# A one-token decode layer on one core: Tile framework against a recorder, load pieces of 16 to 32 KB against 16 to 64 KB per partition, softmax per kv head against per two kv heads

## The chip, the cores and the metric

The kernel runs on one core of one Trainium2 chip. A core has five engines with an instruction stream each: PE (TensorE, matrix products, writes to PSUM), DVE (VectorE), ACT (ScalarE), POOL (GpSimd) and SP (SyncE, which here only issues DMAs). Sixteen DMA engines move data between HBM and SBUF, the on-chip memory of 128 partitions. The metric is device microseconds of one execution; lower is better. Before the change it is 229.72 us, the median of 3 runs (229.62 to 229.88).

## The reference

One token passes through a parallel layer: layer norm, attention over the last 4096 positions of a cache with 32 query heads on 4 kv heads, and a gated MLP. All is float32.

```python
W = min(4096, max(256, Sk // 4))                     # 4096
xn = _layernorm(x)                                   # (1, 1, 1024)
q = (xn @ wq).reshape(B, Sq, 32, 128)                # wq 1024 x 4096
k = repeat(k_cache[:, :, Sk - W:, :], 8)             # 4 kv heads x 4096 x 128
v = repeat(v_cache[:, :, Sk - W:, :], 8)
p = softmax(q k^T * 128 ** -0.5)
a = (p v).reshape(B, Sq, 4096) @ wo                  # wo 4096 x 1024
h = gelu_tanh(xn @ w_gate) * (xn @ w_up)             # both 1024 x 3584
out = x + a + h @ w_down                             # w_down 3584 x 1024
```

Each weight and each cached key and value is used once, so about 94.4 MB pass from HBM to SBUF.

## The kernel before

All loads are issued by SP in one order (`items`, L75 to L79): four pieces of wq, then k, gate, v and up pieces mixed, then four of wo and four of w_down. A piece fills one of four buffers `chunk` of 32 KB per partition (L55, `load`, L88). Piece n + 4 is loaded into the buffer of piece n, so its DMA on SP waits until PE and DVE have read the whole of piece n (L449). A k or v piece holds two kv heads in two DMAs of 16 KB per partition; a gate or up piece has 28 KB; the last two pieces of w_down are cut finer, down to two DMAs of 2 KB per partition (`TAIL`, L30, and `cuts`, L101).

A projection by a vector (q, gate, up) is done in two halves of the rows: `blocks` (L193) gives half of them to PE as products with a stationary operand of 32 columns, of which one holds x, so that four products stand in four strips of 32 PSUM partitions; `add_scaled` (L181) gives the other half to DVE, which multiplies a row of weights by one number per partition and adds it to `part`. `projected` (L210) sums `part` over the partitions on PE, with `unit`. A q piece of 32 KB is thus one row of 4096 for PE and one for DVE.

Keys: `transpose_keys` (L235) transposes 128 x 128 blocks on PE into two PSUM buffers in turn, four blocks at a time, and ACT copies each group of four to `kT`. `scores` (L245) forms a head's scores as 4 strips x 2 x 512, takes the maximum per partition and the exponential, once per kv head. `values` (L261) multiplies by v. `maxima`, `factors`, `normalizers` and `heads` (L289 to L337) join the partial softmaxes and spread the result over `oz`. `gelu`, `gated` and `hidden` (L344 to L381) form the MLP's inner row `hz`.

wo and w_down (`contract`, L393): a tile is 1024 columns in 128 partitions; every second tile goes to PE (`accumulate`, L387, four products of 256 columns in four strips of `out_p`), the others to DVE (`out_part`). `out_part` joins on PE at tile 20 of w_down; the last tiles all go to PE. Then one DVE addition writes `y` in partitions 0, 32, 64 and 96, one DMA from ACT stores it (L453, L454), and the Tile framework closes the program (its instructions stand under L474).

The order of the work on each engine is the order of the code (`manual_schedule`, L58, and the loop from L410); the framework adds the waits.

Of the kernel before, what the change touches and what calls it, by code (L numbers as in the profile page):

```python
# [9 lines left out]
F32 = mybir.dt.float32  # L10
# [3 lines left out]
PSUM = bass.MemoryType.PSUM  # L14
# [4 lines left out]
REP = HQ // HKV  # L19
# [3 lines left out]
NJ = D // (2 * P)  # L23
NB = 512
NA = DF // NB
CO = D // 4
TD = DF // P
GROUP = 8

TAIL = {0: 1, 1: 4}  # L30

MERGE = 20
# [3 lines left out]
STREAM = 8192  # L36


@with_exitstack
def tile_decode_layer(  # L40
    ctx: ExitStack,
    tc: tile.TileContext,
    x: bass.AP,
    k_cache: bass.AP,
    v_cache: bass.AP,
    wq: bass.AP,
    wo: bass.AP,
    w_gate: bass.AP,
    w_up: bass.AP,
    w_down: bass.AP,  # L50
    out: bass.AP,
):
    nc = tc.nc
    consts = ctx.enter_context(tc.tile_pool(name="consts", bufs=1))
    stream = ctx.enter_context(tc.tile_pool(name="stream", bufs=4))  # L55
    work = ctx.enter_context(tc.tile_pool(name="work", bufs=1))
    psum = ctx.enter_context(tc.tile_pool(name="psum", bufs=1, space=PSUM))
    ctx.enter_context(tc.manual_schedule())  # L58


    def paired(w, jj):
        return w[2 * P * jj:2 * P * (jj + 1), :].rearrange("(p r) n -> p (r n)", r=2)


    def window(cache, g):
        return cache[0, g, SK - WIN:, :].rearrange("(p j) d -> p (j d)", p=P)

    def grouped(w, a):  # L70
        return w[P * GROUP * a:min(P * GROUP * (a + 1), w.shape[0]), :].rearrange(
            "(p t) n -> p t n", p=P
        )

    items = [("q", jj) for jj in range(NJ)]  # L75
    items += [("k", 0), ("g", 0), ("v", 0), ("g", 1), ("g", 2), ("g", 3)]
    items += [("k", 1), ("u", 0), ("v", 1), ("u", 1), ("u", 2), ("u", 3)]
    items += [("o", a) for a in range(HQ // GROUP)]
    items += [("d", a) for a in range(-(-TD // GROUP))]  # L79
    source = {  # L80
        "q": lambda i: [paired(wq, i)], "g": lambda i: [paired(w_gate, i)], "u": lambda i: [paired(w_up, i)],
        "k": lambda i: [window(k_cache, 2 * i + g) for g in range(2)],
        "v": lambda i: [window(v_cache, 2 * i + g) for g in range(2)],
        "o": lambda i: [grouped(wo, i)], "d": lambda i: [grouped(w_down, i)],
    }
    loaded = {}

    def load(n):  # L88
        kind, i = items[n]
        chunk = stream.tile([P, STREAM], F32, name="chunk")  # L90
        at = 0
        for src in source[kind](i):
            size = math.prod(src.shape[1:])
            dst = chunk[:, at:at + size]
            at += size
            if len(src.shape) == 3:
                dst = dst.rearrange("p (t n) -> p t n", t=src.shape[1])
            step = TAIL.get(len(items) - 1 - n)
            if step:
                for t in range(0, src.shape[1], step):  # L100
                    cuts = 2 if n == len(items) - 1 and t == src.shape[1] - 1 else 1  # L101
                    for cut in range(cuts):
                        cols = slice(cut * D // cuts, (cut + 1) * D // cuts)
                        nc.sync.dma_start(dst[:, t:t + step, cols], src[:, t:t + step, cols])
            else:
                nc.sync.dma_start(dst, src)
        loaded[kind, i] = chunk


    x_rows = work.tile([NJ, 2 * P], F32, name="x_rows")  # L110
    nc.scalar.dma_start(x_rows, x.rearrange("a b (j p) -> (a b j) p", j=NJ))
    x_out = work.tile([P, CO], F32, name="x_out")
    nc.vector.memset(x_out, 0.0)
    nc.scalar.dma_start(x_out[0:P:32, :], x.rearrange("a b (c n) -> (a b c) n", n=CO))

    ident = consts.tile([P, P], F32, name="ident")
    make_identity(nc, ident)
    avg = consts.tile([P, P], F32, name="avg")
    nc.vector.memset(avg, 1.0 / D)

    xz = consts.tile([P, 2, NJ, 32], F32, name="xz")
    nc.vector.memset(xz, 0.0)
    qz = consts.tile([P, HKV, 32], F32, name="qz")
    nc.vector.memset(qz, 0.0)
    hz = consts.tile([P, TD, 32], F32, name="hz")
    nc.vector.memset(hz, 0.0)
    oz = consts.tile([P, HQ, 32], F32, name="oz")
    nc.vector.memset(oz, 0.0)
    unit = consts.tile([P, 32], F32, name="unit")
    nc.vector.memset(unit, 0.0)  # L130
    nc.vector.memset(unit[:, 0:1], 1.0)

    same = consts.tile([P, 4, 32], F32, name="same")
    nc.vector.tensor_add(same[:, 0, :], ident[:, 0:32], ident[:, 32:64])
    nc.vector.tensor_add(same[:, 1, :], ident[:, 64:96], ident[:, 96:128])
    nc.vector.tensor_add(same[:, 2, :], same[:, 0, :], same[:, 1, :])
    for c in (0, 1, 3):
        nc.vector.tensor_copy(same[:, c, :], same[:, 2, :])


    pick = consts.tile([P, REP, 16], F32, name="pick")
    nc.vector.tensor_copy(pick, same[:, 0, 0:REP].unsqueeze(2).to_broadcast([P, REP, 16]))
    low = consts.tile([P, 16], F32, name="low")
    nc.vector.reduce_sum(low, ident.rearrange("p (h s) -> p s h", s=16), axis=AX.X)

    def small(name):
        return psum.tile([P, NB], F32, name=name, tag="tp", bufs=2)

    def layer_norm():
        xt_p = small("xt_p")  # L150
        for r in range(2):
            nc.tensor.transpose(
                xt_p[:, r * NJ:(r + 1) * NJ], x_rows[:, r:2 * P:2], ident[:NJ, :NJ]
            )
        xt = work.tile([P, 2 * NJ], F32, name="xt")
        nc.vector.tensor_copy(xt, xt_p[:, :2 * NJ])
        st = work.tile([P, 8], F32, name="st")
        nc.vector.reduce_sum(st[:, 0:1], xt, axis=AX.X)
        mean_p = small("mean_p")
        nc.tensor.matmul(mean_p[:, 0:1], avg, st[:, 0:1], start=True, stop=True)  # L160
        nc.vector.tensor_copy(st[:, 1:2], mean_p[:, 0:1])
        xc = work.tile([P, 2 * NJ], F32, name="xc")
        nc.vector.tensor_scalar(xc, xt, st[:, 1:2], None, op0=ALU.subtract)
        sq = work.tile([P, 2 * NJ], F32, name="sq")
        nc.vector.tensor_mul(sq, xc, xc)
        nc.vector.reduce_sum(st[:, 2:3], sq, axis=AX.X)
        var_p = small("var_p")
        nc.tensor.matmul(var_p[:, 0:1], avg, st[:, 2:3], start=True, stop=True)
        nc.vector.tensor_scalar(st[:, 3:4], var_p[:, 0:1], EPS, None, op0=ALU.add)
        nc.scalar.activation(st[:, 4:5], st[:, 3:4], AF.Sqrt)  # L170

# [7 lines left out]
        )  # L179

    def add_scaled(total, w, factor, first):  # L181

        if first:
            nc.vector.tensor_scalar(total, w, factor, None, op0=ALU.mult)  # L184
        else:
# [292 lines left out]
```

## Time and profile before

| What | us or share |
|---|---|
| device time, median of 3 runs | 229.72 |
| span of the profiled execution, first to last instruction | 228.1 |
| time outside the span (median less span) | 1.6 |
| PE busy, 1096 matrix instructions | 126.9 (56%) |
| DVE busy, 103 instructions | 97.0 (43%) |
| ACT busy, 57 instructions | 33.8 (15%) |
| data moved by DMA | 94.53 MB |
| granted TensorE clock, mean | 0.79 |

Sums over engines do not bound the time: PE, DVE and the DMA engines work side by side. The page cuts the span in 40 slices and gives for each the busy share of every engine and of the DMA engines; a table of windows gives the same for any stretch. The waits of SP tell when a load could not be issued because its buffer was still being read. The profile has no separate time for the profiled execution, so its span of 228.1 us and 1.6 us around it stand for it.

### The profile page before, as it was taken

To read this page: it belongs to the slowest core of one execution; us is meant where nothing else is said; L and a number is where in the kernel's file an instruction comes from. 1 tells how busy PE (TensorE), PEld (TensorE's weight loads), DVE (VectorE), ACT (ScalarE), POOL (GpSimd) and SP (SyncE) were. 2 spreads that over 40 slices of the span, in tenths; PEclk is the share of its full clock that TensorE was granted. 3 is DMA by queue.
4 is the path that set the end of the run, shared out by engine and by line. 5 is a ranking of instruction groups with operands and counts; after the bars stand their busy time and mean duration, and the time that the engine had idled before them with its cause. 6 is when DMAs were issued, how large, how long until landed. Compare 5 with 4: busy or idle time off the path is not lost.

```text
span 228.1 us, 2497 instructions
## 1 busy us (share of the span) xinstructions
PE 126.9 (56%) x1096; PEld 62.8 (28%) x1096; DVE 97.0 (43%) x103; ACT 33.8 (15%) x57; POOL 0.7 (0%) x6
## 2 busy tenths in 40 slices
PE   1160623567939874169806985384895426062754
PEld 1110100154436540017305472110481202021321
DVE  7340724510110564260380327966717356292600
ACT  2000000035065310006416350000000000000000
POOL 1000000000000000000000000000000000000000
PEclk9999999979776998556975899959776655555879
DMA  7999999999999999999999999999999999999990
GB/s 277 455 402 431 460 431 402 428 459 410 424 425 450 410 442 425 413 427 450 415 419 458 417 429 435 422 455 419 417 448 428 414 448 437 419 431 411 418 380 36
DMA packets 4787, 94.53 MB, mean 414 GB/s; under 512 B 541, under 2 KB 553, under 8 KB 1193
## 3 DMA queue, kind: packets, MB, share of 16 engines
q1 hardware_dynamic: 4752, 94.37, 97.0%
q8 instruction: 8, 0.13, 0.2%
q10 hardware_dynamic: 24, 0.01, 0.0%
q14 instruction: 3, 0.02, 0.0%
HBM read 94.38 MB, written 0.00 MB: 414 GB/s over the span
## 4 chain that ended last, share of the span: by engine, by line
DMA 56%; PE 24%; DVE 11%; ACT 5%; issue 2%; SPq 0%; ACTq 0%; DVEq 0%
DMA chunk<-in_A_k_cache 22%; DMA chunk<-in_A_wo 15%; DMA chunk<-in_B_w_down 15%; PE kt_p L241 10%; DMA chunk<-in_A_wq 5%; PE o_p L278 3%; DVE part L186 3%; PE s_p L250 3%; PE out_p L389 3%; PE acc_q L196 2%; DVE out_part L186 2%; DVE m L253 2%; ACT p L256 2%; ACT kT L242 1%; ACT pT L273 1%
## 5 line engine op out<-in xcount | busy, mean ns | idle before, releaser
L186 DVE SCALAR_TENSOR_TENSOR part<-chunk,xz,part 128x3584 f32<-128x3584 f32 (+1 forms) x9 | 37.1, 4126 | 29.4 <-DMA chunk<-in_A_wq 17.8
L241 PE MATMUL kt_p<-ident,chunk 128*128 128x128 f32 x128 | 25.5, 374 | 15.4 <-ACT kT L242 12.3
L242 ACT ACTIVATE kT<-kt_p 128x512 f32<-128x512 f32 x32 | 18.8, 596 | 68.9 <-PE kt_p L241 68.4
L196 PE MATMUL acc_q<-chunk,xz 128*32 128x512 f32 x64 | 14.2, 1040 | 23.7 <-DMA chunk<-in_A_wq 23.7
L241 PEld LDWEIGHTS kt_p<-ident,chunk 128*128 128x128 f32 x128 | 20.2, 192 | 25.2 <-ACT kT L242 15.9
L389 PE MATMUL out_p<-chunk,hz 128*32 128x256 f32 x160 | 14.7, 528 | 16.2 <-DMA chunk<-in_B_w_down 16.2
L186 DVE SCALAR_TENSOR_TENSOR out_part<-chunk,oz,out_part 128x1024 f32<-128x1024 f32 x15 | 19.3, 1285 | 9.7 <-DMA chunk<-in_A_wo 9.3
L389 PE MATMUL out_p<-chunk,oz 128*32 128x256 f32 x128 | 14.2, 621 | 15.3 <-DMA chunk<-in_A_wo 15.3
L196 PE MATMUL acc_g<-chunk,xz 128*32 128x512 f32 x56 | 10.5, 785 | 9.6 <-DMA chunk<-in_B_w_gate 9.6
L253 DVE TENSOR_REDUCE m<-s_p 128x1 f32<-128x1024 f32 x4 | 4.9, 1222 | 23.3 <-PE s_p L250 23.3
L186 DVE SCALAR_TENSOR_TENSOR out_part<-chunk,hz,out_part 128x1024 f32<-128x1024 f32 x8 | 10.3, 1285 | 9.2 <-DMA chunk<-in_B_w_down 8.9
L389 PEld LDWEIGHTS out_p<-chunk,hz 128*32 128x32 f32 x160 | 6.7, 146 | 24.6 <-DMA chunk<-in_B_w_down 12.3
L389 PEld LDWEIGHTS out_p<-chunk,oz 128*32 128x32 f32 x128 | 5.5, 164 | 23.2 <-DMA chunk<-in_A_wo 18.0
L196 PEld LDWEIGHTS acc_q<-chunk,xz 128*32 128x32 f32 x64 | 2.5, 158 | 34.2 <-DMA chunk<-in_A_wq 23.3
L196 PE MATMUL acc_u<-chunk,xz 128*32 128x512 f32 x56 | 9.3, 708 | 3.1 <-DMA chunk<-in_B_w_up 3.1
L250 PE MATMUL s_p<-kT,qz 128*32 128x512 f32 x64 | 10.1, 709 | 0.0
L278 PE MATMUL o_p<-chunk,pT 128*32 128x128 f32 x256 | 7.8, 274 | 1.9 <-ACT pT L273 1.9
L184 DVE TENSOR_SCALAR part<-chunk,xz 128x3584 f32<-128x3584 f32 (+1 forms) x3 | 6.5, 2169 | 3.9 <-DMA chunk<-in_A_wq 3.9
L278 PEld LDWEIGHTS o_p<-chunk,pT 128*32 128x32 f32 x256 | 6.7, 110 | 2.8 <-ACT pT L273 2.8
L196 PEld LDWEIGHTS acc_g<-chunk,xz 128*32 128x32 f32 x56 | 2.1, 125 | 16.2 <-DMA chunk<-in_B_w_gate 12.2
L256 ACT ACTIVATE p<-s_p,negm 128x1024 f32<-128x1024 f32 x4 | 4.5, 1114 | 8.3 <-DVE negm L254 8.3
L350 DVE TENSOR_TENSOR t_sb<-g_sb 128x512 f32<-128x512 f32 (+1 forms) x2 | 1.4, 686 | 9.9 <-ACT g_sb L349 9.9
(93 smaller groups left out, 73.7 us busy)
## 6 DMA issues: line engine op xcount, KB each, us to landing
chunk<-in_A_wq SPq DMA_DIRECT2D x4, 4096.0 KB, 30.8
chunk<-in_A_wo SPq DMA_DIRECT2D x4, 4096.0 KB, 27.8
chunk<-in_B_w_gate SPq DMA_DIRECT2D x4, 3584.0 KB, 17.8
chunk<-in_B_w_up SPq DMA_DIRECT2D x4, 3584.0 KB, 16.7
chunk<-in_A_k_cache SPq DMA_DIRECT2D x4, 2048.0 KB, 26.9
chunk<-in_A_v_cache SPq DMA_DIRECT2D x4, 2048.0 KB, 28.6
chunk<-in_B_w_down SPq DMA_DIRECT2D x2, 4096.0 KB
chunk<-in_B_w_down SPq DMA_DIRECT2D x2, 2048.0 KB, 30.9
```

The source lines that it names most:

```text
L184: nc.vector.tensor_scalar(total, w, factor, None, op0=ALU.mult)
L186: nc.vector.scalar_tensor_tensor(total, w, factor, total, op0=ALU.mult, op1=ALU.add)
L196: nc.tensor.matmul(acc[kind][32 * c:32 * c + 32, b, :], z, w[:, n * NB:(n + 1) * NB], start=start, stop=stop,)
L241: nc.tensor.transpose(t_p[:, jj * P:(jj + 1) * P], kn[:, j * DH:(j + 1) * DH], ident)
L242: nc.scalar.activation(kT[:, i, :], t_p, AF.Copy)
L250: nc.tensor.matmul(s_p[32 * c:32 * c + 32, b, :], qz[:, g, :], kT[:, i, :], start=True, stop=True)
L253: nc.vector.reduce_max(m[:, g:g + 1], s_p, axis=AX.XY)
L256: nc.scalar.activation(p, s_p, AF.Exp, bias=negm[:, g:g + 1], scale=SCALE, accum_out=l[:, g:g + 1])
L273: nc.scalar.activation(pT[:, b].rearrange("p j q -> p (j q)"), t_p, AF.Copy)
L278: nc.tensor.matmul(o_p[32 * c:32 * c + 32, g, :], pT[:, b, jj, 32 * c:32 * c + 32], vn[:, j * DH:(j + 1) * DH], start=(b == 0 and jj == 0) ...
L350: nc.vector.tensor_mul(ts, gs, gs)
L389: nc.tensor.matmul(out_p[32 * c:32 * c + 32, :], z, w[:, c * CO:(c + 1) * CO], start=start, stop=stop)
```

## The change

The Tile framework goes. A class `Program` records every operation with its engine and the boxes (tensor, partitions, range of elements) that it reads and writes, finds for each the latest earlier operation of every other engine or DMA that it has to wait for, and emits the engines' streams with these waits. Engines count on one semaphore each; every DMA has its own. The code's order remains the order on each engine.

Loads go to one ring of 152 KB per partition at fixed places (`pieces`): q, o in two pieces of 64 KB each, gate and up in two of 56 KB, a k piece is one kv head (16 KB), a v piece two kv heads in one DMA (32 KB), w_down 48, 32, 16 KB and four tiles of 4 KB, the last in two halves. A piece is issued on SP as soon as the pieces that lie on its place have been used; pieces are issued in the listed order.

A 64 KB q piece is four rows of 4096: rows 0 and 2 go to PE, 1 and 3 to DVE. Of a gate or up piece one row of four goes to PE, three to DVE. In heads 0 and 1 the copies of key groups 2 and 5 go to DVE, the others to ACT. Scores of two kv heads accumulate in one PSUM bank, 32 rows to a strip (8 heads x 2 kv heads x 2 halves), with `qz` padded so that each product fills its own 8 rows; maximum, exponential and the transposition of the probabilities are then done once for two kv heads. A product of `values` has 512 columns (4 x 128) and `heads` picks each row's own 128 with a masked weight. `hidden` makes its row with two products and a masked sum in place of 36 small products. The program lists 406 matrix operations where it listed 630.

For wo and w_down a PE tile is two products of 512 columns in two strips; tiles alternate between the two pairs of strips. The last two tiles of w_down, `out_part` and the accumulated strips are joined in `final`, in strips of 128 columns x 2 halves, so that the result lies in partitions 31, 32, 95 and 96. Each half has its own addition and two stores, from SP and ACT. At the end SP waits for the four stores and clears the semaphores.

The diff, cut to its core:

```diff
-    stream = ctx.enter_context(tc.tile_pool(name="stream", bufs=4))
...
+RING = 152 * KB
...
+    def emit(self):
...
+        for op in self.ops:
+            engine = self.engines[op["engine"]]
+            waits = [(sems[self.ops[o]["lane"]], self.ops[o]["rank"]) for o in op["waits"]]
+            for sem, value in waits[1:]:
+                engine.wait_ge(sem, value)
+            inst = op["emit"](engine)
+            if waits:
+                inst.wait_op(waits[0][0], waits[0][1], "sem-ge")
...
+    pieces = [
+        ("q", 0, 0, 64), ("q", 1, 72, 64), ("k", 0, 136, 16), ("k", 1, 56, 16), ("g", 0, 0, 56),
+        ("v", 0, 56, 32), ("g", 1, 88, 56), ("k", 2, 0, 16), ("k", 3, 16, 16), ("u", 0, 32, 56),
+        ("v", 1, 0, 32), ("u", 1, 88, 56), ("o", 0, 0, 64), ("o", 1, 64, 64),
+        ("d", (0, 12), 0, 48), ("d", (12, 20), 48, 32), ("d", (20, 24), 80, 16),
+        ("d", (24, 25), 128, 4), ("d", (25, 26), 132, 4), ("d", (26, 27), 136, 4),
+        ("d", (27, 28), 140, 4),
+    ]
...
+    def project(kind, a, on):
+        n = NQ if kind == "q" else NG
+        w = held[kind, a].rearrange("p (r n) -> p r n", r=4)
+        for r in range(4):
+            if r in on:
+                on_pe(kind, xz[:, r, a, :], w[:, r, :], n)
+        for r in range(4):
+            if r not in on:
...
+                add_scaled(part[:, :8 * n], w[:, r, :], xz[:, r, a, 0:1], first)
+        done(kind, a)
...
+    def transpose_keys(g, groups, by):
+        kn = held["k", g]
+        for i in groups:
+            t_p = small()
+            for jj in range(4):
+                j = 4 * i + jj
+                transpose(t_p[:, jj * P:(jj + 1) * P], kn[:, j * DH:(j + 1) * DH], ident[:])
+            copy(kT[:, i, :], t_p[:], by(i))
+        done("k", g)
...
+    def softmax(a):
+        reduce_max(m[:, a:a + 1], s_p[:])
+        scalar_op(negm[:, a:a + 1], m[:, a:a + 1], -SCALE, None, ALU.mult)
+        act(p[:], s_p[:], AF.Exp, bias=negm[:, a:a + 1], scale=SCALE, accum=l[:, a:a + 1])
...
+    def final(half, wide, w, start, stop):
         for c in range(4):
...
+            odd = c % 2
+            mm(
+                acc[32 * c:32 * c + 32, half, :P], wide[:, 31 * odd:31 * odd + 32],
+                w[:, c * P:(c + 1) * P], start, stop,
             )
...
+    project("q", 0, {0, 2})
+    project("q", 1, {0, 2})
+    by = lambda i: "dve" if i in (2, 5) else "act"
+    transpose_keys(0, range(8), by)
+    projected("q")
+    queries()
+    scores(0)
+    transpose_keys(1, range(8), by)
+    scores(1)
+    softmax(0)
+    project("g", 0, {0})
+    transpose_probs()
+    values(0)
...
+    for half in range(2):
+        final(half, unit, out_part[:, half * NQ:(half + 1) * NQ], True, False)
+    copy(acc_sb, out_acc[:], "act")
+    for half in range(2):
+        final(half, half_sel[:, half, :], acc_sb, False, False)
...
+        final(half, hz_last[:, 1, :], w[:, half * NQ:(half + 1) * NQ], False, True)
+        add(y[:, half, :], acc[:, half, :P], x_out[:, half, :])
+        for k, engine in enumerate(("sp", "act")):
+            src = y[31 + 64 * k:33 + 64 * k, half, :]
...
+    for sem in ends:
+        nc.sync.wait_ge(sem, 16)
...
+    nc.sync.sem_clear(range(numbers[0], numbers[-1] + 1))
```

Three places of the streams bear on what follows. The first is SP's stream from the last loads of wq to the first of v; `chunk` is one of the four buffers, the names in brackets are semaphores. Before:

```order
L106 DMA chunk<-in_A_wq 128x8192 x4
L106 DMA chunk<-in_A_k_cache 128x4096 [waits DMAHW1_49,DVE_49,PE_49]
L106 DMA chunk<-in_A_k_cache 128x4096
L106 DMA chunk<-in_B_w_gate 128x7168 [waits DMAHW0_49,DMAHW3_49,DVE_49,PE_49]
L106 DMA chunk<-in_A_v_cache 128x4096 [waits DMAHW4_49,DVE_49,PE_49]
L106 DMA chunk<-in_A_v_cache 128x4096 [waits DMAHW2_49]
```

Now, from the second piece of wq on, with `ring` the one buffer and `s_dve`, `s_pe` the engines' counts:

```order
L192 DMA ring<-in_A_wq 128x16384
L192 DMA ring<-in_A_k_cache 128x4096
L192 DMA ring<-in_A_k_cache 128x4096 [waits s_dve]
L192 DMA ring<-in_B_w_gate 128x14336 [waits s_pe]
L192 DMA ring<-in_A_v_cache 128x2x4096 [waits s_pe]
L192 DMA ring<-in_B_w_gate 128x14336
```

The first load of v waited for the reader of a wq piece four pieces back; now it lies on part of the place of k's head 1 (56 to 72 KB), so it waits for PE's last transposition of that head.

The second place is DVE's stream around the keys of heads 0 and 1. Before, two rows for the last two wq pieces, then the queries and the first softmax:

```order
L186 SCALAR_TENSOR_TENSOR part<-chunk,xz,part 128x4096 [waits DMAHW4_49,DVE_49]
L186 SCALAR_TENSOR_TENSOR part<-chunk,xz,part 128x4096 [waits DMAHW5_49,DVE_49]
L223 COPY qz<-q_p 128x2x8 [waits PE_49] x2
L253 TENSOR_REDUCE m<-s_p 128x1 [waits PE_49]
L254 TENSOR_SCALAR negm<-m 128x1 [waits DVE_49]
```

Now, with `tp` a PSUM buffer of transposed keys:

```order
L186 SCALAR_TENSOR_TENSOR part<-ring,xz,part 128x4096 [waits s_dma5,s_dve]
L186 SCALAR_TENSOR_TENSOR part<-ring,xz,part 128x4096 [waits s_dve]
L159 COPY kT<-tp 128x512 [waits s_pe] x2
L159 COPY rows_sb<-acc 128x512 [waits s_pe]
L159 COPY qz<-tp 128x8 [waits s_pe]
L159 COPY qz<-tp 128x8 x3
L159 COPY kT<-tp 128x512 [waits s_pe] x2
L174 TENSOR_REDUCE m<-s_p 128x1 [waits s_pe]
```

Both DVE rows of the second wq piece now wait for one landing (`s_dma5`), and two copies of transposed keys of each head stand on DVE behind them.

The third place is the end of PE's stream. Before, the last three tiles of w_down, each a product of 256 columns in four strips:

```order
L389 MATMUL out_p<-chunk,hz 32x256 [waits DMAHW7_49]
L389 MATMUL out_p<-chunk,hz 32x256 x3
L389 MATMUL out_p<-chunk,hz 32x256 [waits DMAHW0_49]
L389 MATMUL out_p<-chunk,hz 32x256 x3
L389 MATMUL out_p<-chunk,hz 32x256 [waits DMAHW1_49]
L389 MATMUL out_p<-chunk,hz 32x256
L389 MATMUL out_p<-chunk,hz 32x256 [waits DMAHW2_49]
L389 MATMUL out_p<-chunk,hz 32x256
```

Now, from tile 25 of w_down on:

```order
L134 MATMUL out_acc<-ring,hz 32x512 [waits s_dma516]
L134 MATMUL out_acc<-ring,hz 32x512
L134 MATMUL acc<-kT,unit 32x128 [waits s_dve]
L134 MATMUL acc<-kT,unit 32x128 x7
L134 MATMUL acc<-kT,half_sel 32x128 [waits s_act]
L134 MATMUL acc<-kT,half_sel 32x128 x7
L134 MATMUL acc<-ring,hz_last 32x128 [waits s_dma517]
L134 MATMUL acc<-ring,hz_last 32x128 x7
L134 MATMUL acc<-ring,hz_last 32x128 [waits s_dma518]
L134 MATMUL acc<-ring,hz_last 32x128 x3
L134 MATMUL acc<-ring,hz_last 32x128 [waits s_dma519]
L134 MATMUL acc<-ring,hz_last 32x128 x3
```

Between tile 25 and tile 26 now stand the joining of `out_part` (`unit`) and of the strips (`half_sel`), the latter behind a copy on ACT (`s_act`); each half of the last tile is four products of 128 columns.

More of the change, by code (lines that the diff above doesn't have):

```diff
@@ L35 @@
 GELU_C = math.sqrt(2.0 / math.pi)
[L36 to L54, printed above, removed]
-    stream = ctx.enter_context(tc.tile_pool(name="stream", bufs=4))
[L56 to L62, printed above, removed]
+KB = 1024 // 4
@@ L79, in tile_decode_layer @@
[L79 to L107, printed above, removed]
@@ new lines, in decode_layer, with pump, done @@
+    queue = list(pieces)
+    live = {}
+    def pump():
+        while queue:
+            kind, i, at, size = queue[0]
+            if any(at < hi and lo < at + size for lo, hi in live.values()):
+                return
+            load(*queue.pop(0))
+            live[kind, i] = (at, at + size)
+    def done(*key):
+        del live[key]
+        pump()
+    x_rows = sbuf("x_rows", 2, 512)
+    dma("act", x_rows[:], x.rearrange("a b (c n) -> (a b c) n", c=2), writes=[x_rows[:]])
+    x_out = sbuf("x_out", P, 2, P)
@@ new lines, in decode_layer @@
+    layer_norm()
+    project("q", 0, {0, 2})
[11 more added lines that the diff above has]
+    values(0)
+    project("g", 1, {0})
+    act_only = lambda i: "act"
+    transpose_keys(2, range(8), act_only)
+    scores(2)
+    transpose_keys(3, range(8), act_only)
```

754 lines of the change are left out of this document (450 added, 304 removed).

## The prediction, made before the changed kernel was run

> **What bounds the kernel now.** I read the page's totals and slices first, then the windows by stage, then SP's own waits, then the timeline at two places: where a load could come late, and the end.
>
> ```profile
> span 228.1 us, 2497 instructions
> ...
> DMA  7999999999999999999999999999999999999990
> GB/s 277 455 402 431 460 431 402 428 459 410 424 425 450 410 442 425 413 427 450 415 419 458 417 429 435 422 455 419 417 448 428 414 448 437 419 431 411 418 380 36
> DMA packets 4787, 94.53 MB, mean 414 GB/s; under 512 B 541, under 2 KB 553, under 8 KB 1193
> ...
> q1 hardware_dynamic: 4752, 94.37, 97.0%
> q8 instruction: 8, 0.13, 0.2%
> ```
>
> The DMA engines are busy 90% or more in every slice but the first and the last, and SP's queue alone takes 97.0% of sixteen engines' span. So the kernel ends when 94.37 MB have come, plus what follows the last byte. Every saving elsewhere is worth nothing, and every load that SP issues too late costs in full.
>
> ```profile
> core 0: us, PE busy (x) PEld busy (x) DVE busy (x) ACT busy (x) POOL busy (x), PEclk, DMA share, GB/s
> 0.00:13.00 13.00, 1.51 (x6) 1.31 (x6) 5.97 (x29) 1.49 (x2) 0.70 (x6) 1.00 0.89 364
> 44.00:50.00 6.00, 4.17 (x27) 2.53 (x20) 2.75 (x1) 1.48 (x3) 0.00 (x0) 0.87 1.00 426
> 189.00:205.00 16.00, 7.28 (x64) 2.99 (x64) 10.28 (x8) 0.00 (x0) 0.00 (x0) 0.50 1.00 432
> 216.00:220.00 4.00, 1.46 (x24) 0.54 (x20) 0.00 (x0) 0.00 (x0) 0.00 (x0) 0.89 0.96 391
> ```
>
> The last column by the share gives the rate of busy engines: 432 GB/s with rows of 32 KB, 426 with 16 KB, 407 (391 / 0.96) with 4 KB. Per engine (a sixteenth) a row then takes 1.214, 0.615 and 0.161 us. Taking the slope of the first two, 0.599 us per 16 KB, a row costs some 16 ns beside its bytes; the 4 KB row gives 11 ns. I use 14. The first window holds 4.73 MB, which 430 GB/s would take 11.0 us for: the flow begins in effect 2.0 us after the span's start.
>
> **Packets.** The 528 packets that are no rows (33 loads, one mark on each of 16 engines; the page's 541 under 512 B bear it out) leave 4224 rows before. After, there are 24 loads' worth of 128 rows (each v piece counts twice), 3072. That is 72 rows less per engine, 72 x 14 ns = **1.0 us less**. No trace shows a row of 48 to 64 KB. If the hardware cuts such rows at 32 KB, 64 of the 72 come back (32 rows of 64 KB, 32 of 56 KB give one more each), and the gain is 0.1; at 16 ns it is 1.2. Nearest is the 32 KB row, which moves as one, so I take 1.0.
>
> The 8 instruction packets of 16 KB are fetched code on the same engines. With 406 matrix operations for 630 I expect about 5; three fewer, each worth a 16 KB row on one of sixteen engines (0.6 us), save 0 to 0.6 at the end, depending on which engine ends last: 0.2.
>
> **Loads that may be late.** A load now waits for larger pieces, so each needs its margin.
>
> ```profile
> SPq L106 <- DVE part L186: 60.8, 9, 9.6
> SPq L106 <- PE kt_p L241: 40.6, 2, 20.5
> SPq L474 <- DMA out_y<-y: 27.1, 1, 27.1
> ```
>
> Before, SP waits for readers often, but four pieces stand queued and the flow never breaks. After, the critical one is the first v load: it waits for PE's last transposition of head 1. What is queued ahead of it then is gate piece 0. Two q pieces (16.78 MB), two k (4.19) and gate (7.34) are 28.31 MB; at 430 GB/s that lasts until 2.0 + 65.8 = 67.8 us. From SP's first issue to the effective start (2.0) went 1.3, so the load has to be issued by **66.5 us**; gate piece 1, which needs no wait of its own, stands behind it on SP.
>
> ```profile
> 0.74 2.09 SPq L106 DMA_DIRECT2D chunk<-in_A_wq  x4
> 42.27 4.48 DVE L186 SCALAR_TENSOR_TENSOR part<-chunk,xz,part 128x4096 f32<-128x4096 f32 x1 [5.23 <-DMA chunk<-in_A_wq]
> 47.11 1.09 PE L241 MATMUL kt_p<-ident,chunk 128*128 128x128 f32 x8 [1.58 <-DMA chunk<-in_A_k_cache]
> 49.61 0.60 ACT L242 ACTIVATE kT<-kt_p 128x512 f32<-128x512 f32 x1 [0.72 <-PE kt_p L241]
> 53.40 1.93 PE L196 MATMUL acc_q<-part,unit 128*32 128x512 f32 x16
> 56.47 1.06 PE L219 MATMUL q_p<-ident,q_sb 128*128 128x4 f32 x8 [1.14 <-ACT q_sb L215]
> 58.77 3.57 PE L250 MATMUL s_p<-kT,qz 128*32 128x512 f32 x16
> 66.96 5.57 PE L241 MATMUL kt_p<-ident,chunk 128*128 128x128 f32 x24 [3.59 <-ACT kT L242]
> 72.45 1.93 PE L250 MATMUL s_p<-kT,qz 128*32 128x512 f32 x16
> ```
>
> Two rows by shape, of DVE operations on 512 columns (their last numbers are busy us and mean ns):
>
> ```profile
> L351 DVE TENSOR_SCALAR t_sb<-t_sb 128x512 f32<-128x512 f32 x1 | 0.4, 427 | 0.0
> L360 DVE TENSOR_TENSOR h_sb<-g_sb,acc_u 128x512 f32<-128x512 f32 x1 | 0.7, 686 | 2.0 <-PE acc_u L196 2.0
> ```
>
> The same bytes of wq land, so DVE starts its two rows of piece 1 at 42.3 and ends at 51.2, where it ended at 46.8. PE has groups 0 to 3 of head 0 ready by then, and the copy of group 2 waits for DVE. A DVE copy of 512 columns out of PSUM is not in the trace: at least the 0.43 of L351, which works on SBUF, at most the 0.69 of L360, which reads PSUM as it does; I take 0.69. A group of four transpositions is 0.55 (1.09 / 2), an ACT copy 0.60. From 51.2 in turn: copy 2 to 51.9, group 4 to 52.5, group 5 and copy 4 to 53.1, copy 5 to 53.8, group 7 to 54.4, the join with `unit` (1.93) to 56.3, the queries' two groups of transpositions (0.55 each, 0.3 of waiting) to 57.7, scores of head 0 (1.93) to 59.7. Head 1's eight groups now have two copying engines: two PSUM buffers give 5.0 (four rounds of copy and group, 1.25 each), so PE is done at **64.7**, 1.8 us in time.
>
> The same rows show the other speed of PE: scores took 3.57 at 58.77 and 1.93 at 72.45, and 24 transpositions 5.57, or 6.7 with the first eight. With slow scores and those 6.7 PE is done at 57.7 + 3.6 + 6.7 = 68.0, and the flow breaks for 1.5. I take nothing here, since PE has hardly a gap from 51.9 on, where before it stood 1.1 us for ACT's copy ahead of the slow scores. The Trainium skill, page "TensorE: Matmul & The Clock Gate", section "Part 1: The HAM clock gate", says that the clock halves after an idle window of about 3.4 us and returns after as long a busy one; by that rule PE would keep its full clock here, which is the 64.7.
>
> The other late candidates have room. The second v load waits for both k heads of the second pair: from k 2's landing 6.7 + 3.6 + 6.7 = 17.0, while k 3 and up piece 0 last 4.9 + 17.0 = 21.9 from there; less 1.3, 3.6 us remain. The w_down load of 32 KB waits for DVE's first two tiles of wo piece 1, 1.285 each by this group, against 14.5 us of the 48 KB load ahead of it.
>
> ```profile
> L186 DVE SCALAR_TENSOR_TENSOR out_part<-chunk,oz,out_part 128x1024 f32<-128x1024 f32 x15 | 19.3, 1285 | 9.7 <-DMA chunk<-in_A_wo 9.3
> ```
>
> **The end.**
>
> ```profile
> 180.14 3.64 PE L389 MATMUL out_p<-chunk,oz 128*32 128x256 f32 x32 [6.07 <-DMA chunk<-in_A_wo]
> 214.18 1.94 PE L389 MATMUL out_p<-chunk,hz 128*32 128x256 f32 x32 [1.48 <-DMA chunk<-in_B_w_down]
> 215.93 0.61 PE L389 MATMUL out_p<-out_part,unit 128*32 128x256 f32 x8
> 224.20 0.14 PEld L389 LDWEIGHTS out_p<-chunk,hz 128*32 128x32 f32 x4 [0.27 <-DMA chunk<-in_B_w_down]
> 224.88 0.43 DVE L453 TENSOR_TENSOR y<-out_p,x_out 128x256 f32<-128x256 f32 x1 [10.30 <-PE out_p L389]
> 225.34 0.59 ACTq L454 DMA_DIRECT2D out_y<-y  x1
> ```
>
> And the closing instructions on SP and POOL, with their shortest, median and longest ns:
>
> ```profile
> L474 SPq EVENT_SEMAPHORE  x7: 17/28/28, 227.0 to 228.0; - x7
> L474 POOLq EVENT_SEMAPHORE_RANGE_CLEAR  x1: 96/96/96, 227.7 to 227.7; - x1
> ```
>
> After the last landing PE works 0.7 us (224.20 to 224.88), DVE 0.43, and the store takes from 225.34 to SP's notice at 227.0; then 1.1 us of marks, drains and the clearing pass. Now the last half is four products of 128 columns side by side where half a tile was two of 256: 0.2 less. The addition has 128 columns for 256: 0.1 less. The store costs the same, half of it issued earlier by the same two queues. The end is four waits (28 ns each, three of them met early) and one clearing (0.10): **1.0 less**; if every engine still had to meet at the end, 0.
>
> More stands on PE ahead of it. Behind tile 25 come tile 26 and two halves, 1.05 MB or 2.6 us at the 407 above. In that time PE has tile 25 (four tiles 1.94; in two strips of four a tile alone takes twice its share, 0.97), two joins of 0.61 with ACT's copy of 0.60 between, tile 26 (0.61) and the first half (0.30): 3.1 if the first join hides the copy, so PE is late by up to 0.5. I take **0.3 more**. On the slow clock (3.64 for 1.94) it would be late by some 2.
>
> **Sum.** 228.1 - 1.0 - 0.2 - 0.2 - 0.1 - 1.0 + 0.3 = 225.9 us of span, with 1.6 around it **227.5**. The profiled execution's own time is not shown; 228.1 + 1.6 is the median 229.7, so the sum is against that.
>
> **Rivals.**
> 1. The first v load late, by part of the 1.5 above or somewhat more: 228 to 229.5. For it: PEclk 0.87 to 0.50 in the windows; against it: the unbroken work.
> 2. Slower than before: the same place with PE slow from the first group on. Groups 4 to 7 at 0.93 each (5.57 / 6) end at 55.6, the join takes 3.6, queries 2.0, scores 3.6, head 1's groups 7.4: 72.2, a break of 5.7 and 233.2. It decides from 68.7 on, where 2.2 us late eat the whole gain; 69.2 is beyond 0.2%. Against it: before, no stretch was slow throughout.
> 3. PE late at the end on the slow clock: 2.0 in place of 0.3, 229.2.
> 4. The change does not do what it says: rows are cut again, or the program's end stays: 228.4 to 228.5.
> 5. The rows of 64 KB move more slowly. If q and o (33.6 MB, 78 us at 430 GB/s) moved at 418, 2.2 us are lost and the gain is gone; at 402, the lowest slice in the middle, 5.4 us: 232.9. Against it: slices 2 to 7, wq's rows of 32 KB, average 430, and slices 13 to 16, mostly gate's rows of 28 KB, 432. The Trainium skill, page "DMA: Bandwidth & Descriptors", section "Latency and other measured facts", says that rows pitched at large powers of two copy slower, 207 for 214 GB/s at 512 KiB. By it, taken as an estimate for these rows, 3% of 78 us or 2.6 us would go; no run here has such rows.
>
> **How the numbers follow.** Forecast 227.5 (226.4 to 228.0): 55%. Rival 1: 16%. Rival 2: 7%. Rival 3: 8%. Rival 4: 11%. Rival 5: 3%. What a measurement of this kernel can tell from no change is about 0.2%, 229.26 to 230.18. Below lie the forecast, rival 4, most of 1 and half of 3: 81%. Between: the rest of 1 and 3 and a third of 5: 9%. Above: rival 2, most of 5 and what I don't see, 10%. The range for 8 in 10 runs from 226.4, all gains in full, to 229.6, rivals 1 and 3.
>
> **What would show it.** Right: the queue's packets fall to some 3430 (3072 rows and the marks of 22 loads), the last landing comes 1 to 1.5 us earlier, every long window in the middle keeps a DMA share of 0.98 or more, and under 0.5 us lies between the last store's landing and the span's end. Wrong: a window around 68 us with a lower share and SP waiting for PE's transpositions (rivals 1 and 2), DVE's last addition over 1.3 us behind the last landing (rival 3), or slices at q and o below those at gate and up (rival 5).

## The result and the profile after

The changed kernel takes 227.56 us, the median of 4 runs (227.39 to 227.70), beside 229.78 for the kernel before (4 runs, 229.62 to 229.88). The ratio is 0.9903, with a 95% interval of 0.9888 to 0.9917. The forecast was 227.5. The page of the profiled execution (227.54 us):

```profile
span 226.2 us, 1568 instructions
...
DMA  9899899799989999799979998999999999989991
...
DMA packets 3463, 94.48 MB, mean 418 GB/s; under 512 B 367, under 2 KB 383, under 8 KB 1025
...
q1 hardware_dynamic: 3432, 94.38, 97.3%
q8 instruction: 5, 0.08, 0.1%
```

The loads' queue has 3432 packets for 4752, and code five for eight, as forecast. The 7s and 8s in the slices are no gaps: a packet of 64 KB takes 2.4 us and is counted where it starts, so that a slice of 5.7 us may hold one more or one fewer, and the window shares meant as a sign (0.98 or more) can't be read with such rows. What can be read is the queue's share of the whole span, 97.3%, as before (97.0%). Share times span is the time that the mean engine spent on the loads: 221.3 us before, 220.1 after.

The place of the first v load, in the timeline (start, us, then engine, line and operation; in brackets the idle time and what ended it):

```profile
42.01 9.01 DVE L186 SCALAR_TENSOR_TENSOR part<-ring,xz,part 128x4096 f32<-128x4096 f32 x2 [12.48 <-DMA ring<-in_A_wq]
...
50.93 0.68 DVE L159 COPY kT<-tp 128x512 f32<-128x512 f32 x1
...
54.13 1.92 PE L134 MATMUL acc<-part,unit 128*32 128x512 f32 x16
...
57.45 1.92 PE L134 MATMUL s_p<-kT,qz 128*32 128x512 f32 x16
...
64.66 0.38 SPq L192 DMA_DIRECT2D ring<-in_A_v_cache  x1
```

The forecast's chain came nearly step by step: DVE's two rows done at 51.0 (51.2), its copy 0.68 (0.69), the join at 54.1 (54.4), the scores at 57.5 (57.7), the load issued at 64.66 (64.7). Then the end, in the timeline, and the closing instructions by line (ns shortest, median, longest):

```profile
220.87 0.62 PE L134 MATMUL out_acc<-ring,hz 128*32 128x512 f32 x2 [0.23 <-DMA ring<-in_B_w_down]
...
221.76 0.61 PE L134 MATMUL acc<-kT,unit 128*32 128x128 f32 x12
...
221.97 0.60 ACT L146 ACTIVATE kT<-out_acc 128x512 f32<-128x512 f32 x1 [69.66 <-PE out_acc L134]
...
222.62 0.64 PE L134 MATMUL acc<-kT,half_sel 128*32 128x128 f32 x16 [0.26 <-ACT kT L146]
...
223.08 1.06 PE L134 MATMUL acc<-ring,hz_last 128*32 128x128 f32 x32
223.99 0.51 DVE L162 TENSOR_TENSOR kT<-acc,x_out 128x128 f32<-128x128 f32 x2 [4.34 <-PE acc L134]
224.31 0.64 SPq L192 DMA_DIRECT2D out_y<-kT  x2
```

```profile
L671 SPq EVENT_SEMAPHORE  x2: 17/22/28, 226.0 to 226.1; - x2
...
L673 SPq EVENT_SEMAPHORE_RANGE_CLEAR  x1: 88/88/88, 226.1 to 226.1; - x1
```

The last byte lands at 222.9 by the records of the DMA engines (223.7 before). PE waits for a load for the last time at 220.87, for tile 25; from there it runs without another, and its 32 products of the last two tiles start behind the joins, at 223.08. Both halves come ready together, so DVE adds them back to back. From the last landing to SP's notice of the stores at 226.0 are 3.1 us (3.3 before); from there to the span's end 0.2 (1.1 before).

So the span is shorter by 0.9 up to the last landing, 0.1 to 0.2 in the last products, addition and store, and 0.9 in the closing: 1.9. The rest lies outside the span: every run lists its time and its span, and they differ by 1.28 to 1.34 in the four runs of after, by 1.73 to 1.85 in 15 runs of the kernel before that stood beside the first four experiments. The forecast had 1.6 on both sides. These parts add up to 2.4 for the measured 2.22. With 1.73 to 1.85 around it, the profiled execution of the kernel before took some 229.8 to 229.95, 0.05 to 0.17 above its median (an estimate), so the views of before show a little too much.

### The profile page after: what moved, and what is told of

Read it like the earlier page. It is cut to its first block, busy times and chain, and to the rows that moved or that the text cites. A ratio compares the mean times of both kernels' runs of the same rounds, so it can differ in the third digit from the quotient of the medians.

```text
span 226.2 us, 1568 instructions
## 1 busy us (share of the span) xinstructions
PE 101.9 (45%) x662; PEld 38.1 (17%) x662; DVE 117.8 (52%) x127; ACT 24.5 (11%) x42; POOL 0.7 (0%) x6
## 3 DMA queue, kind: packets, MB, share of 16 engines
q1 hardware_dynamic: 3432, 94.38, 97.3%
## 4 chain that ended last, share of the span: by engine, by line
DMA 72%; DVE 14%; PE 10%; ACT 2%; issue 1%; SPq 0%; DVEq 0%
DMA ring<-in_B_w_gate 18%; DMA ring<-in_A_k_cache 13%; DMA ring<-in_A_wo 12%; DMA ring<-in_B_w_down 11%; DMA ring<-in_A_wq 10%; DMA ring<-in_A_v_cache 8%; DVE part L186 5%; PE tp L137 4%; DVE kT L186 3%; PE o_p L134 3%; PE acc L134 2%; ACT kT L146 2%; DVE part L182 1%; DVE rows_sb L168 1%; PE s_p L134 1%
## 5 line engine op out<-in xcount | busy, mean ns | idle before, releaser
L186 DVE SCALAR_TENSOR_TENSOR part<-ring,xz,part 128x3584 f32<-128x3584 f32 (+1 forms) x13 | 53.0, 4074 | 29.6 <-DMA ring<-in_B_w_gate 16.7
L134 PE MATMUL acc<-ring,xz 128*32 128x512 f32 (+1 forms) x128 | 23.9, 902 | 50.3 <-DMA ring<-in_A_wq 27.0
L146 ACT ACTIVATE kT<-tp 128x512 f32<-128x512 f32 x28 | 15.8, 597 | 79.4 <-PE tp L137 79.4
L186 DVE SCALAR_TENSOR_TENSOR kT<-ring,oz,kT 128x1024 f32<-128x1024 f32 x15 | 19.3, 1285 | 6.5 <-DMA ring<-in_A_wo 6.0
L137 PE MATMUL tp<-ident,ring 128*128 128x128 f32 x128 | 19.4, 299 | 5.2 <-DMA ring<-in_A_k_cache 1.7
L134 PE MATMUL out_acc<-ring,hz 128*32 128x512 f32 x68 | 13.2, 802 | 13.7 <-DMA ring<-in_B_w_down 13.7
L134 PE MATMUL o_p<-ring,pT 128*32 128x512 f32 x64 | 12.1, 923 | 11.6 <-DMA ring<-in_A_v_cache 11.6
L137 PEld LDWEIGHTS tp<-ident,ring 128*128 128x128 f32 x128 | 14.7, 149 | 13.0 <-ACT kT L146 4.3
L186 DVE SCALAR_TENSOR_TENSOR kT<-ring,hz,kT 128x1024 f32<-128x1024 f32 x9 | 11.6, 1285 | 8.4 <-DMA ring<-in_B_w_down 8.2
L134 PE MATMUL out_acc<-ring,oz 128*32 128x512 f32 x64 | 9.5, 747 | 14.2 <-DMA ring<-in_A_wo 14.2
```

The lines of the kernel that those rows point to most:

```text
L134: prog.add("pe", lambda e: e.matmul(o, lhsT, rhs, start=start, stop=stop), [lhsT, rhs], [o])
L137: prog.add("pe", lambda e: e.transpose(o, i, eye), [i, eye], [o])
L146: "act", lambda e: e.activation(o, i, func, scale=scale, **kw),
L186: lambda e: e.scalar_tensor_tensor(o, i, factor, other, op0=ALU.mult, op1=ALU.add),
```

## The experiments

The theory going in: the span's gain is the flow's (fewer rows, fewer code packets) and the closing's; the v load is in time with 1.8 us to spare; PE is a little late at the end. Times below stand against 227.56.

**Rows.** Two kernels cut the loads again, to the kernel before's number of rows, and finer. For the loads of 48 to 64 KB:

```diff
-            dma("sp", slot, src, writes=[slot], tag=(kind, i))
+            parts = 2 if size > 32 else 1
+            n = slot.shape[1] // parts
+            for c in range(parts):
+                dst = slot[:, c * n:(c + 1) * n]
+                dma("sp", dst, src[:, c * n:(c + 1) * n], writes=[dst], tag=(kind, i, c))
```

and likewise for the 48 KB load of w_down; the second kernel has four parts.

> The changed kernel with every load of 48 to 64 KB per partition cut into two loads of 24 to 32 KB, same order and places. Theory (a row costs 11 to 16 ns beside its bytes; 264 rows per DMA engine again for 192): 0.8 to 1.2 us slower than the changed kernel, so 228.4 to 228.8 or 0.9935 to 0.996 of the kernel before. Rival (long rows are worth nothing, the gain lies at the end of the program alone): no change, 0.990.

> The same cut into loads of 12 to 16 KB per partition: 408 rows per DMA engine for 192. Theory: 216 rows x 11 to 16 ns, 2.4 to 3.5 us slower than the changed kernel, so 230.0 to 231.0, about three times the step of the cut to 32 KB. Rival: no change, 0.990; a third case is that the marks of the added loads and their issues cost more than the rows, above 231.5.

e1 took 227.98 (227.87 to 228.11), e2 229.41 (229.21 to 230.67): +0.42 for 72 rows more on each engine and +1.85 for 216, 6 and 9 ns a row. Neither theory nor rival: rows count, at about half the price. Of e2's ten runs six lie at 229.2 to 229.5 and four at 230.0 to 230.7. The two pages, e1's and then e2's (profiled at 230.0):

```profile
span 226.6 us, 1586 instructions
...
q1 hardware_dynamic: 4728, 94.38, 97.5%
```

```profile
span 228.7 us, 1615 instructions
...
q1 hardware_dynamic: 7320, 94.38, 97.5%
```

Share times span gives 220.9 and 223.0 against 220.1: the mean engine is busy 0.8 us longer in e1 (about 11 ns a row), 2.9 in e2 (13 ns), close to the forecast's 14. But the end doesn't wait for the mean engine. The chain of waits shows when the load landed from which the end runs on, after and e1:

```profile
195.30 25.53 DMA ring<-in_B_w_down
220.83 0.04 issue
```

```profile
188.52 32.62 DMA ring<-in_B_w_down
221.15 0.04 issue
```

That landing is 0.32 later in e1. Each of the sixteen engines marks a load when it is done with its part, and the load has landed with the last mark. At the last load of all, the first mark is 0.63 later in e1 than in after (222.11 for 221.48), the mean 0.61, the last only 0.38 (223.69 for 223.31). (The marks lie some 0.4 behind the DMA engines' records of the data.) The last lies behind the first by 1.6 us in e1, 1.8 in after and 2.1 in before; this distance is called the lag below.

In the profiled run of e2 PE fell behind earlier. The end runs on from the landing of tiles 20 to 23, for tile 25 in the other two. From its chain:

```profile
220.10 0.04 issue
220.15 3.51 PE out_acc L134 x17
```

PE's clock was granted at 0.50 there until 223.1; in after it was 1.00 from 217.5 on. The last mark came 1.94 later than in after, the run took 2.46 longer: the other 0.5 is rival 3 on a small scale. Whether the same happened in the other three long runs is not recorded.

**The v load's margin.** e3 gives one more row of the second q piece to DVE, to make the load late on purpose:

```diff
-    project("q", 1, {0, 2})
+    project("q", 1, {0})
```

> The second wq piece gives one row of four to PE and three to DVE (two and two before), so DVE frees the keys' copies 4.5 us later and the first v load is issued at about 69.2 us instead of 64.7. Theory (the load had 1.8 us to spare, then the flow breaks and nothing makes it up): 4.5 - 1.8 = 2.7 us slower than the changed kernel, 230.2, between 229.5 and 230.8. Rival (the queue has more behind it than thought, no break): within 0.3 us of the changed kernel. Second rival (the margin was already used up): 4.5 us slower, 232.

231.37 (231.32 to 231.71), ratio 1.0073 [1.0058, 1.0089]: slower than before. From its timeline, then its window from 66 to 72 us (the last three columns are the granted clock, DMA share and GB/s):

```profile
56.14 3.65 PE L137 MATMUL tp<-ident,ring 128*128 128x128 f32 x16 [6.85 <-DVE kT L159]
...
70.24 0.38 SPq L192 DMA_DIRECT2D ring<-in_A_v_cache  x1
```

```profile
66.00:72.00 6.00, 5.22 (x44) 3.30 (x48) 1.38 (x2) 4.14 (x7) 0.00 (x0) 1.00 0.28 91
```

The same window of after:

```profile
66.00:72.00 6.00, 2.25 (x20) 0.50 (x16) 2.64 (x3) 1.34 (x3) 0.00 (x0) 0.89 0.75 321
```

The load was issued 5.58 later than in after and the kernel is 3.81 longer. 1.77 us were free, so the latest moment is 64.66 + 1.77 = **66.4** (forecast 66.5). That it came 5.6 and not 4.5 later is PE's clock: it idled 6.85 us for DVE's copy, the granted clock was 0.50 from 52.6 to 59.4, and the transpositions that followed took 0.91 a group of four for 0.55.

**The closing.** e4 lets all engines meet before and after the clearing of the semaphores, as the framework did:

```diff
+    nc.all_engine_barrier()
     nc.sync.sem_clear(range(numbers[0], numbers[-1] + 1))
+    nc.all_engine_barrier()
```

> The changed kernel with all five engines meeting before and after the clearing of the semaphores, as the kernel before closes. Theory (the shorter end gives 0.9 us): 0.7 to 1.1 us slower than the changed kernel, 228.3 to 228.7. Rival (the meeting lies in time that passes anyway after the stores, outside the span): span longer, time unchanged at 227.6.

228.51 (228.36 to 228.58): +0.95 as expected, but not where expected. The span is 226.7 in the profiled run, 0.5 more, and time less span is 1.78 to 1.91 in the five runs, 0.5 more, that of the kernel before. The closing lines of e4:

```profile
L671 SPq EVENT_SEMAPHORE  x2: 28/28/28, 226.0 to 226.1; - x2
```

```profile
L675 POOLq EVENT_SEMAPHORE  x2: 17/17/17, 226.6 to 226.6; - x2
...
L675 SPq EVENT_SEMAPHORE  x1: 17/17/17, 226.7 to 226.7; - x1
```

SP has its notice at 226.0 in both; the meetings then last until 226.7, and the program is taken as ended 1.8 us after that for 1.3 where PE, DVE, ACT and POOL are done before SP. From the notice to the end are thus 0.7 us in e4, 0.2 in after and 1.1 in before: e4 does not put the whole of the old closing back.

**PE at the end.** e5 takes PE's lateness away: the last four tiles of w_down (not two) are products of 128 columns, and the joins stand ahead of tiles 25 to 27.

```diff
-    tile_on_pe(hz[:, 24, :], held["d", (24, 25)], (True, True))
-    tile_on_pe(hz[:, 25, :], held["d", (25, 26)], (True, True))
     for half in range(2):
         final(half, unit, out_part[:, half * NQ:(half + 1) * NQ], True, False)
     copy(acc_sb, out_acc[:], "act")
+    tail_tile(24)
     for half in range(2):
         final(half, half_sel[:, half, :], acc_sb, False, False)
+    tail_tile(25)
+    tail_tile(26)
```

> The changed kernel with the last four tiles of w_down, not two, multiplied as eight products of 128 columns into the result's strips, and the joins of DVE's sum and of the strips moved ahead, between tiles 23 and 25. Theory (PE is behind the last landing by 0.4 to 0.8 us, and both halves' stores then queue one behind the other for 0.3): 0.4 to 0.9 us faster than the changed kernel, 226.7 to 227.2. Rival (the last landing alone sets the end): no change, 227.6.

226.96 (226.82 to 229.44; five of the six runs up to 227.09), ratio 0.9896 [0.9865, 0.9926]. Its timeline at the end:

```profile
222.77 0.16 PEld L134 LDWEIGHTS acc<-ring,hz_last 128*32 128x32 f32 x8 [0.25 <-DMA ring<-in_B_w_down]
223.26 0.29 DVE L162 TENSOR_TENSOR kT<-acc,x_out 128x128 f32<-128x128 f32 x1 [3.60 <-PE acc L134]
223.40 0.16 PEld L134 LDWEIGHTS acc<-ring,hz_last 128*32 128x32 f32 x8 [0.48 <-DMA ring<-in_B_w_down]
223.41 0.42 PE L134 MATMUL acc<-ring,hz_last 128*32 128x128 f32 x8 [0.21 <-DMA ring<-in_B_w_down]
...
223.90 0.29 DVE L162 TENSOR_TENSOR kT<-acc,x_out 128x128 f32<-128x128 f32 x1 [0.34 <-PE acc L134]
```

Now PE waits for each of the last loads, and the first half's addition begins (223.26) before the last products do (223.41). PE's lateness, and the two halves' additions and stores coming one behind the other, cost 0.6 us together; the run does not part them.

**Engines with room.** Two kernels ask whether DVE's work is on the path. e6 adds three multiplications of 896 columns ahead of `gelu` (`for _ in range(3): mul(ts, gs, gs)`); e7 gives all key copies of heads 0 and 1 to ACT (`by = lambda i: "act"`).

> The changed kernel with three more multiplications of 896 columns on DVE (3.3 us, results not used) ahead of gelu. They delay the second wo load, which has some 4 us to spare. Theory (work off the loads' path is free): within 0.2 us of the changed kernel. Rival (DVE is busy enough, 52%, to bound): up to 3.3 us slower.

> The changed kernel with all key copies of heads 0 and 1 on ACT, none on DVE. Head 0 no longer waits for DVE's rows, head 1 takes 6.7 to 7.4 us for 5.0. Theory: the first v load is issued at 64.5 to 66.5 us, inside its margin; within 0.2 us of the changed kernel. Rival (the two DVE copies are needed): 0.5 us or more slower.

e6: 227.61 (227.45 to 228.22), as after, though DVE ends `hidden` 3.2 us later. e7: 227.38 (227.33 to 227.51); the v load is issued at 63.25, 1.4 earlier, and the time changes by less than 0.2. Work off the flow is free in both directions. e9 joins e5 and e7.

> Both edits in one kernel: the last four tiles of w_down as products of 128 columns with the joins moved ahead of them, and all copies of the first pair's key transpositions on ACT. If the first only takes PE out of the end and the second only relieves DVE, which nothing waits for there, they don't touch each other: 0.6 less than the kernel after from the first and 0 to 0.2 less from the second, 226.8 to 227.0. The v load should be issued at about 63.3, 1.4 earlier, and nothing should come of that, since its place in the queue was already early enough. Rival: the earlier v load counts (a flow that had small gaps there): 226.6 or less.

226.99 (226.71 to 227.09), ratio 0.9873 [0.9855, 0.9890]. So e5's gain stands and e7 adds nothing: 2.8 us below the kernel before, 0.6 below the kernel after.

**Code.** e8 adds 1024 instructions on PE, four groups of 64 products with one column whose results nothing uses: ahead of the first wq piece and behind it, behind the second up piece and behind the first wo piece.

```diff
+    filler()
     project("q", 0, {0, 2})
+    filler()
     project("q", 1, {0, 2})
```

> The changed kernel with four times 64 one-column products on PE in stretches where it waits for wq, up and wo (1024 more instructions, results not used), so 4 more packets of code on the DMA engines: 9 for 5. Theory (part of the gain over the kernel before, some 0.4 us, comes from fetching less code): 0.2 to 0.6 us slower than the changed kernel, 227.8 to 228.2. Rival (code packets cost nothing): within 0.1 us.

228.28 (227.78 to 228.68): +0.72, and nine code packets for five. That looks like a price of 0.18 a packet, but it isn't one. From e8's timeline:

```profile
43.17 5.13 PE L134 MATMUL acc<-ring,xz 128*32 128x512 f32 x32 [8.14 <-DMA ring<-in_A_wq]
...
67.07 0.38 SPq L192 DMA_DIRECT2D ring<-in_A_v_cache  x1
```

The second q piece landed 1.2 us later than in after (41.96), and the v load was issued 0.64 past the latest moment that e3 gives. The flow broke there. So the groups were moved to where PE waits anyway (e10: two behind the first q piece, one behind each wo piece):

> The same 1024 instructions more on PE as in e8, but where PE waits anyway: two groups of 64 products behind the first q piece (PE then idles for 13.8 us) and one behind each wo piece (14.2 and 8.7 us of idling). Their results are used by nothing. In e8 two groups stood ahead of the v load, which was issued at 67.1 for 64.7, past the latest moment of 66.4 that e3 gives: about 0.65 of its 0.72 would be a flow that broke, and not code. Theory: four more code packets cost the mean engine 0.04 to 0.07 each, so +0.1 to +0.3 here (227.7 to 227.9), with the v load issued by 64.8 and nine code packets in the profile. Rival, e8 read as it stands: 0.18 a packet, +0.7 (228.3) here too.

It took 228.93 (227.84 to 229.46, profiled at 229.46), and missed its purpose in the same way. Its timeline:

```profile
43.45 5.82 PE L134 MATMUL acc<-ring,xz 128*32 128x512 f32 x32 [2.66 <-DMA ring<-in_A_wq]
...
67.69 0.38 SPq L192 DMA_DIRECT2D ring<-in_A_v_cache  x1
```

PE waited for the load there, not the load for PE: with two code packets fetched at 34.1 and 41.4, while wq was landing, the piece came 1.5 later, and only on two engines: fourteen of its sixteen marks stand at 41.6 to 42.1 (all sixteen at 41.5 to 41.9 in after), two at 43.3 and 43.4. PE's clock, 0.65 to 0.8 from 53 to 59 us, did the rest.

The marks show what code costs. In e8 one code packet comes at 19.4 and one at 36.4; at the first q piece fifteen marks stand at 22.1 to 22.75 and one at 23.74, at the second fourteen by 42.1 and two at 43.1. So a packet sets one engine back by 1 to 1.5 us, and that engine stays back as long as the flow has no gap. (In e3, behind the broken flow, the lag is down from 1.80 to 0.78.) After has five code packets, the first at 53.4: the lag is 0.43 at the last load that landed before, 1.96 at the next, and at the last load eleven marks stand at 221.5 to 221.8 and five at 222.7 to 223.3.

e11 has all four groups behind the second up piece and the wo pieces, where no load waits for PE within 15 us.

> The same 1024 instructions more on PE, all of them behind the second up piece and the two wo pieces, where PE idles 12.4, 14.2 and 8.7 us and no load waits for it within 15 us. The results are used by nothing. In e10 the two groups ahead of the first key transpositions had their code fetched while wq was landing, the v load came at 67.7, and the flow broke; so neither e8 nor e10 shows the price of the packets alone. Theory: a code packet costs the flow 0.05 to 0.1, so four more give +0.1 to +0.5 (227.7 to 228.1), the v load is issued at 64.6 to 65.0 and no window shows a lower DMA share. Rival: the engine that fetches ends last by the whole of its packets, 0.2 each or more, +0.7 to +1.0 (228.3 to 228.6) with an unbroken flow.

227.51 (227.36 to 228.13): no change, below both ranges. From its page, its timeline, its windows (the granted clock is the third column from the right) and its chain:

```profile
q8 instruction: 9, 0.15, 0.3%
```

```profile
51.78 3.31 PE L137 MATMUL tp<-ident,ring 128*128 128x128 f32 x16 [1.85 <-DVE kT L159]
...
66.01 0.38 SPq L192 DMA_DIRECT2D ring<-in_A_v_cache  x1
```

```profile
53.00:56.00 3.00, 2.92 (x17) 1.90 (x20) 0.69 (x1) 1.26 (x3) 0.00 (x0) 0.50 1.40 598
```

```profile
195.15 25.50 DMA ring<-in_B_w_down
220.65 0.04 issue
```

Four more code packets, and the landing from which the end runs on is 0.18 earlier than in after. At the last load seven marks stand at 221.5 to 221.9 and nine at 222.7 to 223.2: nine engines are set back for five in after, so that the mean mark is 0.39 later, but the last one is where it was (223.22 for 223.31). This run shows something else as well: with the same program up to there, the v load came at 66.0, 0.4 before the latest moment, since PE's clock fell to 0.50 at 53 us, after 1.85 us of idling; in after it stayed at 1.00 there.

## Why the prediction was right, and where two sizes were off

**The bound** was as read: the flow of the loads. Where it broke (e3) the time rose by the gap; more work on DVE (e6) and less (e7) changed nothing.

**The rows** were mis-sized. The forecast took the mean engine's price, 14 ns x 72 = 1.0, for the end's. e1 gives 0.4 in the time. The mean engine's price is nearly right (11 to 13 ns by share times span); the step that failed is that all of it reaches the end, where only the slowest engine counts (0.38 by the last mark, for 0.63 by the first). That the rows stay whole is shown by the 3432 packets, so rival 4's first half fell. Rival 5 fell too: with the 64 KB rows the loads took the mean engine 220.1 us, with the rows of e1 220.9, and by the DMA engines' records a row of 64 KB takes 2.42 us (median) and one of 56 KB 2.12, 27.1 GB/s an engine each, where before one of 32 KB took 1.215 (27.0). The Trainium skill, page "DMA: Bandwidth & Descriptors", section "Latency and other measured facts", gives 207 for 214 GB/s at a row pitch of 512 KiB. The forecast stretched that to these rows, which are 64 KB apart and for which the page gives no figure; the measurement shows no loss here, and it decides.

**The code packets** (0.2, from 0 to 0.6) were the wrong thing to count. Four more (e11) cost the end nothing. The end waits for one of the engines that are set back, however many there are: nine at the last load in before (seven marks at 222.1 to 222.75, nine at 223.4 to 224.2), five in after. Both kernels pay for the first, and three packets fewer do not take that away. The forecast put a packet at 0.6 us on its engine; the records show about 1.0, and the marks 1 to 1.5.

So of the 0.9 by which the last landing came earlier (forecast 1.2), e1 accounts for 0.4. About 0.5 stays open: no run put it back. The marks show where it lies: in e1, with as many rows as before, the first engine is done with the last load when it was before (222.11 and 222.07), but the last lies 1.6 us behind it for 2.1. What makes the lag larger in before was not tried; among seven profiled kernels with the rows of after and an unbroken flow it is 1.7 (e7) to 2.0 us (e9).

**The closing** was put at 1.0, all of it in the span. The views show 0.9 in the span and 0.5 outside; e4 puts 0.95 back, half of it outside. So the mechanism is shown, and the other 0.4 in the span is read from the views alone. The forecast's constant of 1.6 around the span was wrong on both sides: 1.8 before, 1.3 after. This gain of 0.5 that no term had stands against the 0.3 to 0.4 that the landing fell short; that these two cancel is luck, and 227.5 came out right partly by it. In all, e1 and e4 put back 1.37 of the 2.22 us; the causes of the rest are argued and not shown.

**PE at the end**: forecast 0.3 more, up to 0.5; e5 shows 0.6, the stacked additions and stores included. ACT's copy wasn't hidden by the first join: PE waited for it from 222.4 to 222.6, and DVE's two additions and the two store issues on each queue stand one behind the other, which the sum had not. Rival 3's slow clock did not come in after; in the profiled run of e2 it did.

**The v load**: 64.66 for 64.7, latest moment 66.4 for 66.5. Rivals 1 and 2 did not happen, but their weight was fair. In e11 the slow clock took 1.35 of the 1.8 us of margin; a load that came 0.64 late cost 0.7 (e8), one that came 1.26 late 1.9 (e10, profiled runs), where the lag at the end was 2.7 us besides, for 1.8 in after; and e3 is rival 2 in small. Its load at 70.2 makes the kernel 1.6 us slower than before, so the gain is gone from 68.6 on; the forecast's point was 68.7. The Trainium skill, page "TensorE: Matmul & The Clock Gate", section "Part 1: The HAM clock gate", has the clock halved after an idle window of about 3.4 us that runs free of the kernel. e3 agrees (6.85 us of idling, slow after it). In e11 1.85 us of idling sufficed, in e10 1.47, and in after 1.25 did not bring it down: the whole window of idling that the page asks for wasn't needed here.

## What to carry to other kernels

In a kernel that the DMA engines bound, count per load when it must be issued, measure that margin by delaying the load on purpose, and check any experiment for it before its time is read: e8 and e10 measured a late load and not what they were made for. The end is set by the slowest of the sixteen engines, so a saving on the mean engine may arrive only in part, and a single fetch of code sets an engine back for as long as the flow has no gap. Look at time less span as well as at the span: a program whose engines need not meet at the end is shorter there too.

## What the runs showed of the hardware that was not expected

- The time outside the span is no constant: 1.73 to 1.85 us in the kernel before and 1.78 to 1.91 in e4, where all engines meet at the end; 1.26 to 1.45 in all runs of the kernels without a meeting.
- A code packet of 16 KB takes about 1 us on one DMA engine of sixteen, sets that engine back by 1 to 1.5 us, and it does not catch up while loads flow. So the first packet delays every later landing, in e8 and e10 that of the second q piece by 1.2 and 1.5 us; four fetched after the first cost the end nothing (e11).
- The sixteen engines do not end together. Before code is fetched the last lies 0.3 to 0.8 us behind the first; at the last load it is 1.6 (e1) to 2.7 us (e10), with the same number of rows on each.
